# A Fourier transform fused with a soft mixture of experts: another order of the first phase's units

## The chip, the cores and the metric

The kernel runs on one core of a Trainium2 chip. The metric is the device time of one execution in microseconds (us); for a set of runs the median is given. The profiler records one further execution, and all views of the profile below come from that one.

## What is computed

The input `x` has the shape (8, 2496, 256). A two-dimensional discrete Fourier transform is taken over its last two axes and the real part kept; the 19968 rows of the result then go through a soft mixture of experts with 32 slots.

```python
X = np.fft.fft(np.fft.fft(x, axis=1), axis=2).real      # (8, 2496, 256)
x = X.reshape(19968, 256)
logits = x @ phi                                        # (19968, 32)
d = np.exp(logits - logits.max(0)); d /= d.sum(0) + 1e-9
slot_input = (d.T @ x).reshape(8, 4, 256)
for e in range(8):
    slot_out[e] = np.maximum(slot_input[e] @ w1[e], 0) @ w2[e]
c = np.exp(logits - logits.max(1)); c /= c.sum(1) + 1e-9
return c @ slot_out.reshape(32, 256)
```

The full transform is never formed. Only its product with `phi` is needed (2496 x 32 logits for each batch entry), and later the product of the softmax weights with it, so both transforms are applied to narrow matrices. 2496 is 64 x 39, and the transform along that axis is done in two steps, of length 64 and of length 39.

## The kernel before

The eight batch entries are worked on as four pairs, numbered 0 to 3. The work on a pair is cut into units, each a Python function with a letter; two digits behind the letter give the pair and the part. The list `ORDER` (line 34) names the units one after the other, and the loop at line 645 calls them in that order. The calls hand their instructions to a scheduling layer, which then puts the instructions of each engine in a queue; so `ORDER` sets the order of the queues broadly, and the layer may still move single instructions past each other. Every engine works through its queue strictly in order.

Two phases follow each other. The first phase, up to the unit `m00`, reads `x` and makes the logits and the slot inputs; its units are those that the change touches:

- `a` (`part_a`, line 209): one or two of the five loads `x` of a pair. VectorE (DVE) adds the halves of the load (lines 220 and 222) and forms its sum and difference into a tile `eo` (lines 224, 225). TensorE (PE) transposes `eo` in eight blocks into two banks `pt` (line 229), and ScalarE (ACT) copies each bank to a tile `et` (line 230). Unit parts 0 and 1 take two loads each, part 2 one.
- `z` (`part_z`, line 233): PE multiplies the `et` tiles of one `a` unit with `wphi` into a bank `z` (line 244), ACT copies it to `zs` (line 252).
- `t` (line 258): PE transposes the ten blocks of `zs` into `zt` (line 265), ACT copies.
- `b` (line 272): the transform of length 64, eleven products `a` of PE (line 279) and three copies of ACT into `o1` (line 286).
- `c` (line 288), in two halves: the transform of length 39, products `lp` and `lm` (lines 297, 298); ACT copies `lp` (line 299), DVE adds and subtracts `lm` to give the logits `lt` (lines 301, 302) and takes maxima (305). The maxima go through PE (`mt`, line 310), DVE (312, 314), PE again (`mt` out of `mex`, line 315) and DVE (317); then ACT takes the exponentials (320) and DVE forms `dpm` (322, 323).
- `e` (line 326) and `d` (line 346), in two halves each: the two transforms back, products at lines 335 and 353, copied by ACT (344, 359) and for one half of `d` by DVE (359).
- `u` (line 363): four products `tok` (line 366) and forty products with the `eo` tiles (line 376) into one bank `u`.
- `w` queues the loads of the experts' weights on SyncE (SP). They go into slots that `x` and `eo` tiles give up.

The second phase computes the experts (units `m`, `l`, `v`, `r`), the other softmax (`s`, `x`), and the output (`k`, `o`, `g`, `h`).

The products of PE are of different tile shapes, which matters below:

```python
pe.transpose(b[:, g * 128 : g * 128 + 128], e[:, g, k * 128 : k * 128 + 128], ident)   # 229 pt, whole array
z[32 * g : 32 * g + 32, o : o + n], ..., tile_position=(0, 32 * g),                    # 244 z, four strips of 32 columns
ps[64 * k : 64 * k + 64, 120 * i : 120 * i + 120], ..., tile_position=(0, 64 * k),     # 335 e, two halves of 64 columns
```

Using the whole array are `pt`, `zt`, `a`, `lp` and `lm`; four strips of 32 columns each take a part of `z`, `tok` and `u`; two halves of 64 columns take `e` and `d`; the transposes of the maxima `mt` (line 310) write 5 or 6 columns, and the transposes back (line 315) and the product `msel` (line 432) take 5 or 6 rows.

The buffers that bear on the order: `pt` and `z` share two PSUM banks (`P1 = 2`, tag `p1`); `zt`, `a`, `lp` and `lm` share two others (`P2 = 2`, tag `ps`); `mt`, `e`, `d` and `tok` share three (`P3 = 3`); `u` has one. There are three `et` tiles, six slots for `x` (`RING = 6`) and fifteen for `eo`.

Of the kernel before, what the change touches and what calls it, by code (L numbers as in the profile page):

```python
# [31 lines left out]
P1, P2, P3, PM = 2, 2, 3, 0  # L32
W2 = [1, 1, 1, 1, 1, 1, 1, 1, 1, 1, 1, 2, 2, 1]
ORDER = (
# [6 lines left out]
).split()  # L41


# [653 lines left out]
```

## Time and profile before

| | us |
|---|---|
| median of 3 runs | 194.75 |
| lowest and highest of them | 193.83, 195.87 |
| the profiled execution, its own time | 195.39 |
| the profiled execution, span from first to last instruction | 193.6 |
| mean granted clock of TensorE in it | 0.992 |

The time of an execution is a little longer than its span, here by 1.8 us. How much of the span each engine was busy, the span in 40 slices, and the waits are in the views that the prediction shows. To read them: PE is the matmuls of TensorE, PEld its weight loads, DVE VectorE, ACT ScalarE, POOL GpSimd, SP SyncE's queue. `pt<-cs,eo` is an instruction that writes `pt` and reads `cs` and `eo`. In the profile nearly every product of PE that is no transpose stands as two matmuls, so twelve products `z` are "x24", while four transposes `pt` are "x4". In the view of the chain each piece runs from the end of the piece before it to its own end.

### The profile page before, as it was taken

The page shows a single profiled execution, that of the slowest core. Times are in us where ns is not written, and L with a number is a line of the kernel's source. Part 1 is how long each engine was busy: PE and PEld are TensorE (multiplying, and loading weights), DVE is VectorE, ACT ScalarE, POOL GpSimd, SP SyncE. Part 2 cuts the span into 40 slices and gives each one's busy share as a digit, 9 for nine tenths or more (in the row PEclk, how much of TensorE's full clock was granted, in tenths as well). Part 3 has the DMA queues.
Part 4 walks back from the last instruction along what each step waited for, and adds up shares of the span by engine and source line. Part 5 has one row for each costly group of instructions (what it writes and reads, how often), then busy time and mean ns, then how long its engine had stood idle before and what let it go on. Part 6 is the DMA issues. An engine that isn't in the chain of part 4 may idle for free.

```text
span 193.6 us, 4203 instructions
## 1 busy us (share of the span) xinstructions
PE 170.0 (88%) x1682; PEld 108.1 (56%) x1682; DVE 125.3 (65%) x227; ACT 111.0 (57%) x244; POOL 20.9 (11%) x25
## 2 busy tenths in 40 slices
PE   0489899899999989999998999999998998988930
PEld 0376577578676876566873878256544443434410
DVE  0499877899995990742257653760489776985740
ACT  2132586586967485475762852521878595784630
POOL 0000000000000000000000000550054325522000
PEclk9999999999999999999999999999999999999996
DMA  5999999999980299700870698990199899999995
GB/s 179 401 428 411 419 416 422 423 414 413 352 325 7 59 413 416 300 3 3 260 278 8 192 346 273 400 406 20 70 405 368 327 406 413 354 422 397 417 427 229
DMA packets 10994, 59.16 MB, mean 306 GB/s; under 512 B 1376, under 2 KB 1760, under 8 KB 6240
## 3 DMA queue, kind: packets, MB, share of 16 engines
q1 hardware_dynamic: 10976, 58.91, 77.4%
q8 instruction: 13, 0.21, 0.5%
q14 instruction: 5, 0.04, 0.1%
HBM read 38.46 MB, written 20.45 MB: 304 GB/s over the span
## 4 chain that ended last, share of the span: by engine, by line
PE 78%; DVE 6%; ACT 5%; DMA 4%; issue 1%; SPq 1%; POOL 1%; ACTq 0%; DVEq 0%; POOLq 0%
PE po L610 18%; PE pt L229 9%; PE z L244 8%; PE e L335 7%; PE d L353 5%; PE a L279 5%; PE u L376 4%; PE h L477 4%; DMA phi<-phih 4%; PE so L497 4%; PE lT L591 3%; PE lp L297 2%; PE lm L298 2%; PE zt L265 2%; PE cT L530 2%; ACT et L230 2%
## 5 line engine op out<-in xcount | busy, mean ns | idle before, releaser
L610 PE MATMUL po<-rh,lTs 64*128 64x512 f32 x160 | 38.1, 607 | 2.2 <-ACT lTs L594 2.1
L618 DVE COPY o<-po 128x512 f32<-128x512 f32 (+1 forms) x40 | 26.8, 680 | 17.4 <-PE po L610 17.1
L229 PE MATMUL pt<-cs,eo 128*128 128x128 f32 x160 | 26.2, 301 | 7.8 <-DVE eo L224 7.6
L230 ACT COPY et<-pt 128x512 f32<-128x512 f32 x40 | 22.8, 587 | 15.4 <-PE pt L229 15.3
L618 ACT COPY o<-po 128x512 f32<-128x512 f32 x40 | 23.2, 585 | 12.1 <-PE po L610 12.1
L229 PEld LDWEIGHTS pt<-cs,eo 128*128 128x128 f32 x160 | 19.9, 153 | 14.2 <-DVE eo L224 7.6
L610 PEld LDWEIGHTS po<-rh,lTs 64*128 64x128 f32 x160 | 14.3, 186 | 17.0 <-issue 10.2
L222 DVE TENSOR_TENSOR x<-x 128x1024 f32<-128x1024 f32 x16 | 19.4, 1215 | 3.3 <-DMA x<-xh 3.3
L244 PE MATMUL z<-et,wphi 128*32 128x256 f32 (+1 forms) x288 | 16.8, 368 | 2.4 <-ACT et L230 2.4
L547 POOL TENSOR_TENSOR c<-c,cm 128x640 f32<-128x640 f32 x8 | 10.0, 1264 | 69.6 <-DVE cm L546 69.6
L320 ACT ACTIVATE d<-lt,nm 120x128 f32<-120x128 f32 x44 | 13.7, 391 | 3.6 <-DVE nm L317 3.6
L335 PE MATMUL e<-cs,dpm 120*64 120x120 f32 x176 | 13.9, 273 | 0.0
L224 DVE TENSOR_TENSOR eo<-x 128x512 f32<-128x512 f32 x20 | 13.6, 682 | 0.3
L225 DVE TENSOR_TENSOR eo<-x 128x512 f32<-128x512 f32 x20 | 13.6, 679 | 0.0
L244 PEld LDWEIGHTS z<-et,wphi 128*32 128x32 f32 x288 | 8.1, 114 | 9.3 <-ACT et L230 3.9
L335 PEld LDWEIGHTS e<-cs,dpm 120*64 120x64 f32 x176 | 11.4, 136 | 2.4 <-issue 1.8
L279 PE MATMUL a<-cs,zt 128*120 128x128 f32 x88 | 11.8, 279 | 1.0 <-DVE lt L302 0.9
L252 ACT COPY zs<-z 128x512 f32<-128x512 f32 (+1 forms) x12 | 6.2, 513 | 10.4 <-PE z L244 10.4
L376 PE MATMUL u<-eo,ds 128*32 128x129 f32 x320 | 11.5, 275 | 0.1
L557 POOL TENSOR_TENSOR c<-c,cm 128x640 f32<-128x640 f32 x8 | 10.1, 1264 | 13.7 <-DVE cm L556 9.5
L279 PEld LDWEIGHTS a<-cs,zt 128*120 128x120 f32 x88 | 10.4, 183 | 2.1 <-DVE lt L302 1.1
L353 PE MATMUL d<-e,cs 128*64 128x320 f32 x64 | 10.7, 443 | 0.5 <-ACT ds L359 0.5
(91 smaller groups left out, 218.5 us busy)
## 6 DMA issues: line engine op xcount, KB each, us to landing
x<-xh SPq DMA_DIRECT2D x16, 1024.0 KB, 12.3
out<-o SPq DMA_DIRECT2D x13, 1024.0 KB, 4.8
w<-w1h SPq DMA_DIRECT2D x6, 1024.0 KB, 8.2
w<-w2h SPq DMA_DIRECT2D x12, 512.0 KB, 6.5
x<-xh SPq DMA_DIRECT2D x4, 896.0 KB, 11.7
out<-o SPq DMA_DIRECT2D x4, 768.0 KB, 5.1
out<-o SPq DMA_DIRECT2D x5, 512.0 KB, 3.6
w<-w1h SPq DMA_DIRECT2D x4, 512.0 KB, 6.8
```

The costliest lines, as they stand in the source:

```text
L222: v.tensor_tensor(x[:, 0:4], x[:, 0:4], x[:, 4:8], op=ALU.add)
L224: v.tensor_tensor(e[:, :, 0:128], x[:, 0:4, 0:128], x[:, 0:4, 128:256], op=ALU.add)
L229: pe.transpose(b[:, g * 128 : g * 128 + 128], e[:, g, k * 128 : k * 128 + 128], ident)
L230: sc.copy(tr[k][:, :, :, qi, :], b.rearrange("p (g h a) -> p g h a", g=4, h=2))
L244: pe.matmul(z[32 * g : 32 * g + 32, o : o + n], wphi[:, w, :], tr[k][:, g].rearrange("p h q a -> p (h q a)"), start=w != 0, stop=w != 1, t ...
L279: pe.matmul(ps[:120, i * 128 : i * 128 + 128], zt[p][:, GS * g : GS * g + GS].rearrange("p s h c -> p (s h c)"), C("wa"), start=True, stop ...
L320: sc.activation(d[:, g], L[:, g], AF.Exp, bias=nm[:, g : g + 1], scale=1.0)
L335: pe.matmul(ps[64 * k : 64 * k + 64, 120 * i : 120 * i + 120], dpm[p, hf][:, k, 3 * j + i, :], C(name), start=True, stop=True, tile_positi ...
L353: pe.matmul(ps[64 * h : 64 * h + 64, :320], C("wb")[:, 64 * k : 64 * k + 64], esb[p].rearrange("p g (s h c) -> p (g s) h c", h=2, c=NKC)[: ...
L376: last = pe.matmul(ub[32 * g : 32 * g + 32, 0:129], dsb[p][:, k, c, :], e[:, 0:129] if k == 0 else e[:, 127:256], start=cc == 0, stop=cc == 9,
L610: ins = pe.matmul(po[h], lts[p, b, t][rows], rh[0][rows].rearrange("p k d -> p (k d)"), start=True, stop=True, tile_position=(64 * h, 0),)
L618: ins = ev(ot[:np_, 2 * i : 2 * i + 2, :].rearrange("p k d -> p (k d)"), po[h][:np_])
```

## The change

The list `ORDER` is written in another order up to the unit `u30`; what follows `m00` is the same, and so is every function. No unit is added or left out.

```diff
 ORDER = (
-    "a00 z00 a01 z01 a02 z02 t00 a10 z10 b00 a11 z11 c00 c01 e00 e01 d00 a12 z12 t10 a20 z20 a21 z21 "
-    "a22 z22 d01 b10 c10 e10 u00 a30 z30 d10 t20 c11 e11 b20 d11 c20 c21 a31 z31 "
...
+    "a00 z00 a01 a02 z01 z02 a10 t00 z10 b00 c00 c01 e00 d00 a11 a12 z11 z12 a20 e01 z20 d01 u00 t10 "
+    "b10 c10 a21 z21 c11 e10 d10 a22 z22 t20 a30 z30 b20 e11 c20 a31 d11 z31 c21 u10 a32 z32 t30 e20 "
...
 ).split()
```

In the pairs 0 and 1 the units `a` of parts 1 and 2 now stand together, and the units `z` of these parts behind them. Some units `c`, `e`, `d` and `u` of a pair move to other places between the units `a` and `z` of the next.

Three places show what this makes of the queues. In the names the digit straight behind the letters is the pair, the next one the load, half or part; the last number is a running number of the tile and can be passed over.

PE's queue in pair 0, between the loads 3 and 4 and the first transposes of pair 1, before:

```order
L229 MATMUL pt0_3_0_212<-cs0_70,eo0_3_143 128x128 x4
L229 MATMUL pt0_3_1_218<-cs0_70,eo0_3_143 128x128 x4
L244 MATMUL z0_1_224<-et0_1_1_193,wphi_100 32x256 x8
L244 MATMUL z0_1_224<-et0_1_0_192,wphi_100 32x256 x4
L229 MATMUL pt0_4_0_243<-cs0_70,eo0_4_144 128x128 x4
L229 MATMUL pt0_4_1_249<-cs0_70,eo0_4_144 128x128 x4
L265 MATMUL zt0_0_271<-cs0_70,zs0_177 128x128 x2
L265 MATMUL zt0_1_277<-cs0_70,zs0_177 128x128 x2
L244 MATMUL z0_2_255<-et0_2_1_239,wphi_100 32x128 x8
L244 MATMUL z0_2_255<-et0_2_0_238,wphi_100 32x128 x4
L229 MATMUL pt1_0_0_298<-cs0_70,eo1_0_288 128x128 x4
```

and in the changed kernel:

```order
L229 MATMUL pt0_3_0_212<-cs0_70,eo0_3_143 128x128 x4
L229 MATMUL pt0_3_1_218<-cs0_70,eo0_3_143 128x128 x4
L229 MATMUL pt0_4_0_229<-cs0_70,eo0_4_144 128x128 x4
L229 MATMUL pt0_4_1_235<-cs0_70,eo0_4_144 128x128 x4
L244 MATMUL z0_1_241<-et0_1_1_193,wphi_100 32x256 x8
L244 MATMUL z0_1_241<-et0_1_0_192,wphi_100 32x256 x4
L244 MATMUL z0_2_255<-et0_2_1_225,wphi_100 32x128 x8
L244 MATMUL z0_2_255<-et0_2_0_224,wphi_100 32x128 x4
L229 MATMUL pt1_0_0_279<-cs0_70,eo1_0_269 128x128 x4
```

The product `z` of part 1 has moved behind the transposes of load 4 and stands next to the `z` of part 2; two blocks `zt` that stood between them come later.

DVE's queue where the second half of pair 1's logits is formed, before:

```order
L224 TENSOR_TENSOR eo3_3_799<-x3_3_131 128x4x128
L225 TENSOR_TENSOR eo3_3_799<-x3_3_131 128x4x128
L317 COPY nm1_0_719<-mt1_0_713 120x6
L224 TENSOR_TENSOR eo3_4_800<-x3_4_133 128x4x128
L225 TENSOR_TENSOR eo3_4_800<-x3_4_133 128x4x128
L301 TENSOR_TENSOR lt1_703<-lt1_703,lm1_1_877 120x5x64
L302 TENSOR_TENSOR lt1_703<-lt1_703,lm1_1_877 120x5x64
```

and in the changed kernel:

```order
L302 TENSOR_TENSOR lt1_674<-lt1_674,lm1_0_676 120x6x64
L222 TENSOR_TENSOR x3_1_127<-x3_1_127 128x1024
L301 TENSOR_TENSOR lt1_674<-lt1_674,lm1_1_749 120x5x64
L322 TENSOR_TENSOR dpm0_1_409<-d0_1_403 120x320
L323 TENSOR_TENSOR dpm0_1_409<-d0_1_403 120x320
L305 TENSOR_REDUCE mx1_0_682<-lt1_674 120x6
L302 TENSOR_TENSOR lt1_674<-lt1_674,lm1_1_749 120x5x64
L359 COPY ds0_429<-d0_1_0_434 128x20x16
L222 TENSOR_TENSOR x3_2_129<-x3_2_129 128x1024
```

The two operations that empty the bank of `lm1_1` stood behind the whole preparation of pair 3; now they stand between pair 3's loads 1 and 2.

PE's queue at pair 3's transform of length 64 and of length 39, before:

```order
L279 MATMUL a3_1_1178<-cs2_72,zt3_1090 120x128 x4
L335 MATMUL e2_0_0_1043<-cs3_73,dpm2_0_967 64x120
L335 MATMUL e2_0_1_1051<-cs3_73,dpm2_0_967 64x120
L279 MATMUL a3_2_1184<-cs2_72,zt3_1090 120x128 x3
L335 MATMUL e2_0_0_1043<-cs3_73,dpm2_0_967 64x120 x5
L335 MATMUL e2_0_1_1051<-cs3_73,dpm2_0_967 64x120 x5
L297 MATMUL lp3_0_1199<-o13_1171,cs2_72 120x384
L298 MATMUL lm3_0_1200<-o13_1171,cs2_72 120x384
L335 MATMUL e2_1_0_1109<-cs3_73,dpm2_1_993 64x120
L335 MATMUL e2_1_1_1117<-cs3_73,dpm2_1_993 64x120
L335 MATMUL e2_1_0_1109<-cs3_73,dpm2_1_993 64x120 x5
L335 MATMUL e2_1_1_1117<-cs3_73,dpm2_1_993 64x120 x3
```

and in the changed kernel:

```order
L279 MATMUL a3_0_1158<-cs2_72,zt3_1121 120x128 x4
L279 MATMUL a3_1_1164<-cs2_72,zt3_1121 120x128 x4
L279 MATMUL a3_2_1170<-cs2_72,zt3_1121 120x128 x3
L297 MATMUL lp3_0_1240<-o13_1157,cs2_72 120x384
L298 MATMUL lm3_0_1241<-o13_1157,cs2_72 120x384
L297 MATMUL lp3_1_1284<-o13_1157,cs2_72 120x320
L298 MATMUL lm3_1_1285<-o13_1157,cs2_72 120x320
L310 MATMUL mt3_0_1249<-cs0_70,mx3_0_1247 6x120
L353 MATMUL d2_0_0_1268<-e2_1140,cs2_72 64x320 x2
L353 MATMUL d2_1_0_1272<-e2_1140,cs2_72 64x320 x2
```

The products `e` of pair 2, which stood between pair 3's products, have all moved ahead of them; pair 3's `a`, `lp` and `lm` follow each other without a break.

8 rows, old and new, of the table ORDER are left out of this document.

## The prediction

> **What bounds the kernel now.** I read the page first, for the engine that is busy throughout; then the busy times by stretch, for where it is; then the chain of waits in order of time, for what a change of tile shape costs; last the timeline of PE and the totals of the waits, for what PE waits for. The page:
>
> ```profile
> span 193.6 us, 4203 instructions
> ...
> PE 170.0 (88%) x1682; PEld 108.1 (56%) x1682; DVE 125.3 (65%) x227; ACT 111.0 (57%) x244; POOL 20.9 (11%) x25
> ...
> PE   0489899899999989999998999999998998988930
> ...
> DVE  0499877899995990742257653760489776985740
> ```
>
> PE is busy 88% of the span and in nearly every slice. DVE is as full only up to the fifteenth slice (72 us). The change ends at PE's first `cT` (117.6 us in the chain below); I split what lies ahead of that where the same PE work is done by both orders: behind pair 2's first `z` (49.2 us) and behind pair 3's first `z` (73.5 us). Columns: length, then busy time with the number of instructions for PE, PEld, DVE, ACT, POOL, then granted clock, DMA share, GB/s.
>
> ```profile
> 7.60:49.20 41.60, 38.69 (x353) 28.56 (x353) 36.36 (x55) 24.36 (x50) 0.26 (x2) 1.00 1.02 415
> 49.20:73.50 24.30, 23.44 (x297) 17.69 (x293) 21.32 (x36) 16.82 (x43) 0.13 (x1) 1.00 0.62 237
> 73.50:117.60 44.10, 43.00 (x591) 30.40 (x587) 19.98 (x54) 25.69 (x72) 0.00 (x0) 1.00 0.54 193
> 117.60:193.60 76.00, 64.91 (x452) 31.47 (x450) 45.94 (x81) 42.81 (x79) 20.09 (x16) 0.98 0.84 338
> ```
>
> In the first stage the loads run at 415 GB/s with the DMA engines full, and DVE, which must prepare each load, is busy 36.36 of 41.60 us: PE is fed. In the second, PE and DVE are both nearly full (23.44 and 21.32 of 24.30). In the third DVE has more than half its time free, and PE alone sets the pace (43.00 of 44.10). The fourth the change does not touch.
>
> PE's busy time hides a cost that the chain shows (start, length, what; each length is from end to end):
>
> ```profile
> 30.95 0.65 PE lp L297 x2
> ...
> 46.27 0.66 PE a L279 x6
> ...
> 51.58 0.44 PE pt L229 x4
> 52.02 0.55 PE e L335 x4
> 52.57 0.59 PE pt L229 x4
> 53.16 1.37 PE e L335 x20
> ...
> 92.08 1.02 PE u L376 x32
> ...
> 95.93 0.84 PE a L279 x6
> ...
> 98.15 0.83 PE lp L297 x2
> ...
> 101.75 0.54 PE lm L298 x2
> 102.29 1.23 PE d L353 x8
> 109.80 2.60 PE e L335 x42
> 112.40 2.27 PE d L353 x16
> 115.24 2.39 PE u L376 x76
> 117.63 0.56 PE cT L530 x4
> ```
>
> The same four transposes take 0.44 us behind other whole-array work and 0.59 behind an `e`: a change of shape costs 0.15. Likewise `a`: 0.84 - 0.66 = 0.18; `lp`: 0.83 - 0.65 = 0.18. For the others I compare a short group with a long one. `e`: 22 matmuls more cost 2.60 - 1.37 = 1.23, or 56 ns each; so 20 would take 1.12, and entering costs 0.25; for the group of four 0.55 - 0.22 = 0.33. `d`: eight more cost 1.04, so entering costs 1.23 - 1.04 = 0.19. `u`: 44 more cost 1.37, 31 ns each, so 32 take 1.00 and entering seems free by this; since that division has a rounding of its own, I bound it by 0 and by the 0.19 of `d`, and take the middle, 0.10, for all strips.
>
> The Trainium skill, "TensorEngine Tiling (Array Packing)", section "Key Properties", says that changing the tiling mode, not just the tile, drains the TensorE. This trace agrees in direction (0.59 against 0.44 us). The page gives no price; "TensorE: Matmul & The Clock Gate", section "Step-by-step: what each phase is for", puts the drain at about 128 cycles, 53 ns at 2.4 GHz, so an estimate from that page for 14 changes would be -0.7 us. The rows above measure more.
>
> What PE waits for, in the timeline (the last bracket is the idle time before, and who ended it), and the waits in total:
>
> ```profile
> 21.73 1.50 PE L244 MATMUL z<-et,wphi 128*32 128x256 f32 x24 [0.73 <-ACT et L230]
> 25.32 0.86 PE L244 MATMUL z<-et,wphi 128*32 128x128 f32 x24 [0.29 <-ACT et L230]
> 37.33 1.50 PE L244 MATMUL z<-et,wphi 128*32 128x256 f32 x24 [0.68 <-ACT et L230]
> 71.26 0.92 PE L279 MATMUL a<-cs,zt 128*120 128x128 f32 x6 [0.86 <-DVE lt L302]
> 82.13 0.22 PE L315 MATMUL mt<-cs,mex 5*120 5x5 f32 x1 [0.17 <-DVE mex L314]
> 82.62 0.41 PE L265 MATMUL zt<-cs,zs 128*128 128x128 f32 x2 [0.27 <-DVE nm L317]
> 101.59 0.70 PE L298 MATMUL lm<-o,cs 120*120 120x320 f32 x2
> 104.93 0.76 PE L353 MATMUL d<-e,cs 128*64 128x320 f32 x4 [0.52 <-ACT ds L359]
> ...
> 20.60 1.07 ACT L230 COPY et<-pt 128x512 f32<-128x512 f32 x2 [0.61 <-PE pt L229]
> 34.84 0.43 ACT L299 COPY lt<-lp 120x320 f32<-120x320 f32 x1 [0.60 <-PE lp L297]
> ...
> DVE lt L301 <- PE lm L298: 8.9, 5, 5.0
> ...
> PEld h L477 <- DMA w<-w2h: 0.9, 3, 0.3
> ```
>
> **The change, part by part.** It adds and removes no instruction. I went down PE's queue and counted the rows whose kind of tile differs from the row before (whole array; strips; halves; `mt`; transposes back and `msel`), as far as the first `cT`: 85 changes before, 71 now. By stage 21 and 17, 18 and 20, 46 and 34.
>
> *First stage.* Four changes less: at `pt` three, at `z`, `zt` and `lp` one each, against two more at `a`; 3 x 0.15 + 0.10 + 0.15 + 0.18 - 2 x 0.18 = 0.52 us of PE's work. The waits of `z` for ACT's copies in pairs 0 and 1 (0.73 and 0.68) go too, since the transposes of load 4 now stand between. But those transposes now follow load 3's straight on. They share two banks, ACT needs 1.07 / 2 = 0.54 us to empty one and PE 0.44 to fill one, so PE waits there some 0.1 each time; and the second `z` straight behind the first must wait for an `et` tile, of which there are three: the copy into it (0.54) starts only when the first `z` has read the old content, so some 0.5 where 0.29 was. The `zt` blocks and pair 1's next transposes stand behind these copies and come late by 0.3 to 0.4 each. More important, the loads and DVE give the pace of this stage, and neither starts sooner: an `x` slot is freed by DVE alone, and DVE's queue over pairs 0 and 1 starts the same. I take this stage at 0, with bounds -0.5 and +0.5.
>
> *Second and third stage.* Ten changes less (64 to 54): at `a` two less, `lm` two, `e` two, and at the strips six (`z` one, `u` two, `tok` three); one more at `pt` and at `d`. That is 0.36 + 0.36 + 2 x 0.29 (middle of 0.25 and 0.33) + 6 x 0.10 - 0.15 - 0.19 = 1.56 us off PE's work. If entering the strips is free it is 0.96; at 0.19 it is 2.10.
>
> Waits that go: the 0.86 us at 71.26, because DVE now empties pair 1's last `lm` bank before it prepares the end of pair 3 and not after; 0.17 + 0.27 at 82, because pair 1's maxima are done earlier; and 0.52 at 104.93, where `d` waited for ACT's copy of the bank before, and now a transpose and `msel` stand between. Sum 1.82.
>
> Waits that come: pair 3's `a`, `lp` and `lm` now follow each other without the `e` that stood between. They have two banks, so a product waits for the copy of the one before the last. The second `lm` waits for the second `lp` to end (0.70, taken from the `lm` of the same size at 101.59) and for ACT's copy of it (0.43), less the 0.54 in which PE is done with it in the chain (row 101.75): 0.6. The same reckoning at the first `lp` and the second `lp`, where more stands between, gives 0.1 to 0.2 each; and `mt` behind them waits for DVE's chain on that `lm`, some 0.4. Sum 1.3. All of it is on the path, as PE alone sets the pace there. What hid it before, twelve products `e`, is used up earlier.
>
> Sum: 0 - 1.56 - 1.82 + 1.3 = -2.1 us. The last stage moves up with it: its weight loads are issued when `u` gives up its `eo` tiles, and the `u` units move up as well, so I cost the SP queue at nothing; the weights' cover would be gone if the last loads arrived later than their products, and now the longest wait for them is 0.3 us (last row above). The sum stands against the profiled execution's own 195.39 us (span 193.6), which is 0.6 above the median: 193.3 there, and 194.75 - 2.1 = 192.6 on the median.
>
> **The rivals.** *The new waits eat most of it.* In the first stage and at pair 3, units that share two banks now follow each other. If at pair 3 each of the three waits for a copy finds ACT just taken by another of 0.43, that is 1.3 more: -0.8, 193.9. For it speaks that ACT's copy (0.54) is longer than PE's group (0.44); against it that ACT is busy only 25.69 of 44.10 us in the third stage. The Trainium skill, "Perfetto Trace Analysis", section "Matmuls", bears on it: independent matmul groups should rotate through different banks so that the emptying of one overlaps the next group. With two banks that is just met, and no run here shows yet what a third would give.
>
> *The gain is larger.* If the first stage does keep its 0.52 and the waits of `z` (1.41), because DVE has 5.2 us free in it, then -2.1 - 1.9 = -4.0: 190.7. For it: PE's busy share there is 93%. Against it: a DMA share of 1.02.
>
> *Slower.* DVE's additions for pair 1's logits now stand ahead of pair 3's additions in its queue, so if PE brings `lm` late, DVE stands still with pair 3's loads behind it. DVE's waits for `lm` were 8.9 us in five, the longest 5.0. DVE has 24.30 - 21.32 = 3.0 us free in the second stage; from a wait of 3.0 on, the rest is on the path. With one of 5.0 that is +2.0, and the 1.82 of waits come back: -2.1 + 3.8 = +1.7, 196.5. Against it: pair 1's second `lm` now stands well ahead in PE's queue, before that pair's `mt`.
>
> That the change doesn't do what it says is excluded: the queues show 14 changes of shape less, and the chain that a change has a price.
>
> **How the numbers follow.** The forecast has 0.60, the first rival 0.22, the larger gain 0.12, the slower case 0.06. What a measurement of this kernel can tell from no change is about 1%, 1.9 us: under 192.8 is faster, over 196.7 slower. The forecast's own range is 191.4 to 193.9 (strips free or at 0.19; first stage at -0.5 or +0.5), and somewhat more than half of it lies under 192.8: 0.34. With the larger gain and a little of the first rival that is 0.48 faster; slower is the upper half of the slow case, 0.04; the same 0.48. To leave two in ten out, the range takes in the first rival and part of the larger gain: 191.2 to 194.5.
>
> **What would show it.** In the profile after: the transposes of load 4 in pairs 0 and 1 without a `z` ahead of them, and those `z` without idle time before them; the second `z` of pair 0 with about 0.5 us idle; no wait of `a` for `lt`; at pair 3 the second `lm` with about 0.6 us idle. The stretch from pair 2's first `z` to the first `cT`, 68.4 us now, should be 66.3. If instead the stretch up to pair 2's first `z`, 41.6 us, is shorter by more than 1 us, the first stage was not set by loads and DVE; if idle time at pair 3 exceeds 2 us, the first rival holds; if DVE shows a wait for `lm` over 3 us between pairs 1 and 3, the slow one.

## The result, and the profile after

The changed kernel takes 192.24 us (median of 4 runs, 191.79 to 192.42), the kernel before 195.08 (4 runs, 193.83 to 195.87): ratio 0.985, 95% interval 0.981 to 0.989. Each median here and below is over all executions of a kernel, while the ratios leave out those more than 1.5% above its fastest (one of 4 of `u_whole`, three of 12 of `h4_start_alone`, and five of 12 of `b1_third_bank`, whose profile is of one of the five). The profiled execution of the changed kernel took 191.79 us with a span of 190.0. Its page:

```profile
span 190.0 us, 4194 instructions
...
PE 166.9 (88%) x1682; PEld 104.8 (55%) x1682; DVE 125.9 (66%) x227; ACT 110.8 (58%) x244; POOL 20.9 (11%) x25
```

PE does the same 1682 instructions in 3.1 us less busy time (it was 170.0). Where, the busy times of the changed kernel by stretch show (columns as in the prediction; cut behind pair 2's first `z`, behind pair 3's first `z`, and at the first `cT`):

```profile
7.70:48.50 40.80, 37.90 (x353) 27.54 (x353) 36.38 (x55) 24.43 (x51) 0.27 (x2) 1.00 1.02 418
48.50:72.20 23.70, 23.57 (x310) 17.20 (x306) 20.85 (x38) 16.75 (x45) 0.13 (x1) 1.00 0.62 222
72.20:114.00 41.80, 40.46 (x578) 28.61 (x574) 20.00 (x53) 25.50 (x72) 0.00 (x0) 1.00 0.59 218
114.00:190.00 76.00, 64.98 (x453) 31.50 (x450) 46.95 (x81) 42.87 (x79) 20.12 (x16) 0.98 0.84 338
```

The first stage is 0.8 us shorter than before, the second 0.6, the third 2.3, the last the same. The second cut is not at the same work: in the changed kernel twelve products (eight `tok`, two `lp`, two `mt`) have moved from the third stage into the second, so these two can only be read together, and the same holds for what the prediction and some expectations say of them singly. In the second and third together PE is busy 64.03 us where it was 66.44, that is 2.41 less, and idle 1.47 where it was 1.96, that is 0.49 less. Most of the gain is thus in PE's own rows, not in its waits. By line, the groups of PE in these two stages, first before and then after (busy us, mean ns of one, idle time ahead):

```profile
L335 PE MATMUL e<-cs,dpm 120*64 120x120 f32 x176 | 13.9, 273 | 0.0
L376 PE MATMUL u<-eo,ds 128*32 128x129 f32 x320 | 11.5, 275 | 0.1
...
L279 PE MATMUL a<-cs,zt 128*120 128x128 f32 x44 | 6.2, 283 | 0.9 <-DVE lt L302 0.9
```

```profile
L335 PE MATMUL e<-cs,dpm 120*64 120x120 f32 x176 | 12.3, 272 | 0.1
L376 PE MATMUL u<-eo,ds 128*32 128x129 f32 x320 | 11.2, 275 | 0.1
...
L279 PE MATMUL a<-cs,zt 128*120 128x128 f32 x44 | 5.5, 276 | 0.0
```

The products themselves are no faster (273 and 272 ns); `e` alone lies in fewer pieces and takes 1.6 us less, `a` 0.7, `u` 0.3.

The waits of PE in the changed kernel's timeline:

```profile
21.22 1.50 PE L244 MATMUL z<-et,wphi 128*32 128x256 f32 x24 [0.15 <-ACT et L230]
23.05 0.86 PE L244 MATMUL z<-et,wphi 128*32 128x128 f32 x24 [0.33 <-ACT et L230]
25.67 0.44 PE L265 MATMUL zt<-cs,zs 128*128 128x128 f32 x2 [0.29 <-ACT zt L267]
42.66 0.48 PE L279 MATMUL a<-cs,zt 128*120 128x128 f32 x2 [0.74 <-ACT zt L270]
...
90.96 0.44 PE L265 MATMUL zt<-cs,zs 128*128 128x128 f32 x2 [0.38 <-ACT zs L252]
98.11 0.80 PE L298 MATMUL lm<-o,cs 120*120 120x320 f32 x2 [0.52 <-ACT lt L299]
99.17 0.27 PE L310 MATMUL mt<-cs,mx 120*6 120x120 f32 x1 [0.26 <-DVE mx L305]
```

The wait of `a` for `lt` (0.86), those at 82 us and that of `d` (0.52) are gone. New in the third stage are a wait of `zt` for ACT's copy to `zs` (0.38) and, at pair 3, those of the second `lm` and the `mt` behind it, 0.52 and 0.26.

### The profile page after: what moved, and what is told of

Read it like the earlier page. It is cut to its first block, busy times and chain, and to the rows that moved or that the text cites. A ratio compares the mean times of both kernels' runs of the same rounds, so it can differ in the third digit from the quotient of the medians.

```text
span 190.0 us, 4194 instructions
## 1 busy us (share of the span) xinstructions
PE 166.9 (88%) x1682; PEld 104.8 (55%) x1682; DVE 125.9 (66%) x227; ACT 110.8 (58%) x244; POOL 20.9 (11%) x25
## 4 chain that ended last, share of the span: by engine, by line
PE 73%; ACT 12%; DVE 5%; DMA 3%; issue 2%; POOL 1%; SPq 0%; ACTq 0%; DVEq 0%; POOLq 0%
PE po L610 18%; PE pt L229 9%; PE z L244 8%; PE a L279 6%; PE d L353 5%; ACT d L320 4%; PE h L477 4%; PE e L335 4%; PE so L497 4%; ACT et L230 3%; PE u L376 3%; PE lT L591 3%; DMA x<-xh 3%; PE lp L297 2%; PE lm L298 2%; PE cT L530 2%
## 5 line engine op out<-in xcount | busy, mean ns | idle before, releaser
L229 PE MATMUL pt<-cs,eo 128*128 128x128 f32 x160 | 25.7, 293 | 8.1 <-DVE eo L224 7.7
L229 PEld LDWEIGHTS pt<-cs,eo 128*128 128x128 f32 x160 | 19.3, 149 | 13.9 <-DVE eo L224 7.7
L335 PE MATMUL e<-cs,dpm 120*64 120x120 f32 x176 | 12.3, 272 | 0.1
L335 PEld LDWEIGHTS e<-cs,dpm 120*64 120x64 f32 x176 | 10.1, 136 | 2.5 <-issue 0.8
```

Source lines behind the costliest of these rows:

```text
L335: pe.matmul(ps[64 * k : 64 * k + 64, 120 * i : 120 * i + 120], dpm[p, hf][:, k, 3 * j + i, :], C(name), start=True, stop=True, tile_positi ...
```

## The experiments

For the kernels that move units alone, the table shows changes of shape up to the first `cT`, the stretch from pair 2's first `z` to the first `cT` in the profiled execution, and a split of it: I took the usual time from the start of one product to the start of the next, which makes 53.26 us in every kernel; what the first and last products at a change of shape take beyond that is "changes", all else "waits". The split is my reckoning from the start times in the traces.

| kernel | changes of shape | stretch, us | of it changes, waits | ratio to before (95% interval) |
|---|---|---|---|---|
| before | 85 | 68.29 | 12.07, 2.96 | |
| the changed kernel | 71 | 65.49 | 9.80, 2.43 | 0.985 (0.981 to 0.989) |
| h1_group_alone | 85 | 68.92 | 11.90, 3.76 | 1.006 (1.004 to 1.008) |
| h2_no_group | 76 | 65.92 | 10.50, 2.16 | 0.987 (0.985 to 0.989) |
| h3_rest_alone | 77 | 67.87 | 10.65, 3.96 | 1.003 (0.999 to 1.006) |
| h4_start_alone | 81 | 68.04 | 11.09, 3.69 | 1.005 (1.001 to 1.009) |
| h6_e_back | 67 | 66.17 | 8.92, 3.99 | 0.994 (0.991 to 0.997) |
| s1_other_order | 72 | 64.55 | 9.05, 2.24 | 0.990 (0.985 to 0.994) |

**The price of a change, by itself.** Nine products of one column in the shape of the whole array were put into pair 3's `u`, between its ten groups of four products; they write a column that nobody reads, and the copy of `tok` moves behind them. The control has the same nine in the shape of `u`.

```diff
             for cc in range(10):
+                if cc and p == NPAIR - 1:
+                    with tc.issue_after(last.ins):
+                        last = pe.matmul(ps[:, 8:9], ident, C("onehot"), start=True, stop=True)
```

> The changed kernel with nine added small products (one column each) in pair 3's u, one ahead of each group of four u products but the first, in whole-array shape; they write an unused column. Nothing else stands in PE's queue there. Theory 'price of a change of shape': each of them brings two changes, 18 in all, at 0.10 to 0.19 us each, so pair 3's u takes 1.8 to 3.4 us longer than with the same nine products in strip shape. Rival 'shape is free, only waits count': no more than 0.3 us longer than with strips.

> The control: the changed kernel with the same nine added small products at the same places of pair 3's u, but in the shape of one strip, as u itself has. Both theories: only their own issue, some 0.05 us each, 0.3 to 0.9 us in all above the changed kernel.

> As u_whole, but three of the one-column products in the shape of the whole array inside pair 3's u, not nine: 6 changes of shape more where u_whole had 18. u_whole lengthened pair 3's u by 4.3 us against its control, or 0.24 us for a change with its share of the product, and ran slower for some 12 us behind it at a granted clock of 0.58. Theory 'price': pair 3's u is 1.2 to 1.5 us longer than the changed kernel's, and the clock behind it stays at 1.00: ratio 0.990 to 0.995. Rival 'the clock falls after any such product': the stretch behind is longer too, by 2 us or more: ratio 1.003 to 1.015. Rival 'changes inside the strips are nearly free and u_whole's length was the lower clock already': +0.3 us, ratio 0.986 to 0.988.

The control took 193.21 us (ratio 0.989, 0.986 to 0.991), `u_whole` 201.54 (1.031, 1.028 to 1.034), and `u3_whole_sparse`, with three such products (at `cc` 2, 5 and 8), 194.46 (0.996, 0.993 to 0.998). From `tok` to the first `cT` the changed kernel takes 2.93 us, the control 3.29. The timelines of `u3_whole_sparse` and of `u_whole` there:

```profile
111.33 0.24 PE L366 MATMUL tok<-cs,ds 128*32 128x1 f32 x8
...
112.50 0.38 PE L374 MATMUL tok<-cs,cs 128*128 128x1 f32 x2
...
115.61 0.63 PE L534 MATMUL cT<-cs,lt 120*128 120x120 f32 x4
```

```profile
111.98 0.24 PE L366 MATMUL tok<-cs,ds 128*32 128x1 f32 x8
...
117.62 0.38 PE L374 MATMUL tok<-cs,cs 128*128 128x1 f32 x2
...
118.44 0.59 PE L374 MATMUL tok<-cs,cs 128*128 128x1 f32 x2
...
119.55 1.06 PE L534 MATMUL cT<-cs,lt 120*128 120x120 f32 x4
```

Three products lengthen it to 4.28 us, nine to 7.57. Without the 0.36 / 9 = 0.04 us that each takes in the control, that is (1.35 - 0.12) / 6 = 0.20 us a change with six changes, and (7.57 - 3.29) / 18 = 0.24 with eighteen, whose 4.28 us are above the 1.8 to 3.4 expected. The 0.24 holds a lower clock: the last of the nine takes 0.59 us where the one before it takes 0.38, and the granted clock is 0.76 on the mean of 116 to 120 us (last section). The 0.20 is an upper bound, since a product may take longer by itself in the shape of the whole array than in that of one strip, where the control has it. In the lines of `u3_whole_sparse`,

```profile
L374 PE MATMUL tok<-cs,cs 128*128 128x1 f32 x6 | 1.1, 260 | 0.0
```

its two matmuls take 0.26 us each and 0.38 together, so the second starts some 0.12 behind the first, with no change of shape between. With 0.12 for each of the two, (0.45 - 0.24) / 2, about 0.1, is left for a change. Between 0.1 and 0.2 the price stays open; that only waits count (at most 0.3 us for eighteen) falls either way. The other half of the 8.3 us between `u_whole` and its control lies behind this stretch (last section).

**Which part of the order gains.** In `h1_group_alone` the kernel before has only the units `a` of parts 1 and 2 of pairs 0 and 1 together, and their `z` behind them; `h2_no_group` is the changed kernel without that. `h3_rest_alone` has before's order of the units up to the first `u` and the new order of the rest, `h4_start_alone` the reverse.

```diff
-h1: a00 z00 a01 z01 a02 z02 t00 a10 z10 b00 a11 z11 c00 c01 e00 e01 d00 a12 z12 t10
+h1: a00 z00 a01 a02 z01 z02 t00 a10 z10 b00 a11 a12 z11 z12 c00 c01 e00 e01 d00 t10
-h2: a00 z00 a01 a02 z01 z02 a10 t00 z10 b00 c00 c01 e00 d00 a11 a12 z11 z12 a20 e01
+h2: a00 z00 a01 z01 a02 z02 a10 t00 z10 b00 c00 c01 e00 d00 a11 z11 a12 z12 a20 e01
```

> The kernel before with only the grouping put in: in pairs 0 and 1 the units a of parts 1 and 2 stand together and their z behind them; c, e, d and u stay where they were. PE's queue then has 85 changes of shape, as before. Theory 'the grouping of a and z is what gains': 1 us or more below before, under 194. Theory 'the number of changes of shape and the waits of the whole queue count': no gain, 194.5 to 197, as other units fall between others.

> The changed kernel without the grouping: a01 z01 a02 z02 and a11 z11 a12 z12 again, the rest of the new order kept. 76 changes of shape against 71. Theory 'the grouping of a and z is what gains': back to about before, 194.5 to 195.5. Theory 'changes of shape and waits of the whole queue': most of the gain stays, 192.5 to 193.3 (five changes at 0.10 to 0.19, 0.5 to 0.9 us above the changed kernel).

> The kernel before, with the order of its units up to the first u kept, and only the rest (from pair 1's t on) in the new order: 77 changes of shape up to the first cT where the kernel before has 85 and the changed one 71. Theory 'price': 8 changes at about 0.16 us are -1.3 us against the kernel before, about 193.7, ratio 0.993. Rival 'the rest is where the gain is made' (the changed kernel's third stage is 2.2 us shorter than before): about -2.2, 192.9, ratio 0.989. Rival 'the order fits only as a whole' (each half leaves PE waiting for copies and loads that the other half would have brought earlier): within 0.5 us of the kernel before, ratio 0.998 to 1.003.

> The counterpart: the new order up to the first u, and the old order of what is left: 81 changes of shape. Theory 'price': -0.6 us against the kernel before, ratio 0.997. Rival 'the stages add up' (the first two stages of the changed kernel are 0.80 and 0.64 us shorter than before): -0.8 to -1.4, ratio 0.993 to 0.996. Rival 'the order fits only as a whole': -0.2 to +0.6, ratio 0.999 to 1.003.

By the whole time neither the grouping nor either half of the order gains anything by itself: 196.36, 195.82 and 196.84 us. Without the grouping the changed kernel keeps nearly all of its gain (192.66). In the stretch the grouping loses 0.63 us, and the halves keep 0.42 and 0.25 of the 2.80 that the whole order gains. The table says why: each does take something off the changes of shape (0.2, 1.4 and 1.0 us), and each brings waits (0.8, 1.0 and 0.7). The stretch doesn't explain why the whole times of the halves lie above that of the kernel before. For `h3_rest_alone` a lower clock in the last stage bears on it (last section); of `h4_start_alone`, the profiled execution took 194.39 us, like two more of its twelve, and the other nine took 196.3 to 197.3 us, which stays open. The timelines of `h1_group_alone`, of `h3_rest_alone` and of `h4_start_alone` name the waits:

```profile
52.07 1.14 PE L229 MATMUL pt<-cs,eo 128*128 128x128 f32 x8 [0.75 <-ACT et L230]
53.69 0.44 PE L265 MATMUL zt<-cs,zs 128*128 128x128 f32 x2 [0.48 <-DVE lt L302]
70.72 1.14 PE L229 MATMUL pt<-cs,eo 128*128 128x128 f32 x8 [0.56 <-ACT et L230]
```

```profile
55.83 1.50 PE L244 MATMUL z<-et,wphi 128*32 128x256 f32 x24 [0.46 <-ACT et L230]
73.35 1.50 PE L244 MATMUL z<-et,wphi 128*32 128x256 f32 x24 [1.06 <-ACT et L230]
```

```profile
85.32 0.86 PE L244 MATMUL z<-et,wphi 128*32 128x128 f32 x24 [1.08 <-ACT et L230]
...
103.98 0.76 PE L353 MATMUL d<-e,cs 128*64 128x320 f32 x4 [0.53 <-ACT ds L359]
```

Most are waits of `pt` and `z` for ACT's copies to `et`. That the transposes of a load and the `z` on it come too close where old order meets new is how I read these rows; it was not tried by itself. The rival that the order fits only as a whole comes nearest in both halves, and the price alone (-1.3 and -0.6 us) fails as a forecast of the time.

**Fewer changes at the price of waits.** `h6_e_back` puts pair 2's `e` back between pair 3's `b` and `c`, which makes four changes of shape fewer than in the changed kernel.

```diff
-a32 z32 t30 e20 b30 e21 w00 c30 d20 d21 c31 u20
+a32 z32 t30 b30 e20 c30 w00 e21 c31 d20 d21 u20
```

> The changed kernel with the e of pair 2 put back behind pair 3's b and between its two c, and d of pair 2 behind them: only 67 changes of shape where the changed kernel has 71. It keeps PE supplied with other work where the changed kernel waits for the copies of lp (about 1.4 us of waits that came), but zt, a and the first c of pair 3 now follow each other straight on. Theory 'price': 4 changes fewer at about 0.2 us are -0.8 us against the changed kernel, and part of the waits that came goes too, so ratio to the kernel before 0.976 to 0.981. Rival 'waits decide': the a of pair 3 then wait about 1 us for the copies of zt and the first products tok about 1 us for the copies of d, so +1.2 us against the changed kernel, ratio 0.990 to 0.993.

193.75 us, ratio 0.994: slower than the changed kernel, as the rival said, though in the stretch by 0.68 us where it had 1.2. By the table the changes cost 0.88 us less and the waits 1.56 more. In its timeline the wait of `lm` that the `e` was to hide is still there, and two new ones stand beside it:

```profile
92.09 2.72 PE L279 MATMUL a<-cs,zt 128*120 128x128 f32 x22 [0.62 <-ACT zt L270]
97.56 0.80 PE L298 MATMUL lm<-o,cs 120*120 120x320 f32 x2 [0.52 <-ACT lt L299]
...
104.86 0.24 PE L366 MATMUL tok<-cs,ds 128*32 128x1 f32 x8 [0.83 <-ACT ds L359]
```

**The same queue with twelve changes fewer.** In `w1_wide_mt` the transposes `mt` and back are 72 wide, over padding of zeros, and so no longer fit into half of the 128 columns.

```diff
-            pe.transpose(ps[:n, :120], mx, ident[:120, :120])
+            pe.transpose(ps[:WD, :120], mxw, ident[:120, :120])
...
-            pe.transpose(ps[:120, 128 : 128 + n], mex.rearrange("p s k -> p (s k)"), ident[:n, :n])
+            pe.transpose(ps[:120, 128 : 128 + WD], mexw.rearrange("p s k -> p (s k)"), ident[:WD, :WD])
```

> The changed kernel with the same queue of PE, but the twelve transposes of the maxima and back (mt) that write 5 or 6 columns or read 5 or 6 rows made 72 wide by padding the tiles with zeros, which are set once on GpSimd: these products then have the shape of the whole array like the products around most of them, and 12 of the 71 changes of shape go without anything being moved. Theory 'price' at 0.16 us each: -1.9 us against the changed kernel, ratio to the kernel before about 0.975. Rival 'an mt is paid for by a wait anyway' (most mt are waited for: the maxima of VectorE end after PE has come to them, and the wider product takes longer): within 0.4 us of the changed kernel, ratio 0.983 to 0.987.

191.55 us (191.43 to 193.89), ratio 0.986 (0.981 to 0.991); the stretch is 65.15 us, 0.34 less than the changed kernel's for twelve changes. The theory of a price of 0.16 for each change falls here; the rival's size holds. Whether the wider product's own time takes the gain, or a wait that stands there anyway, or whether a narrow `mt` costs no change of shape to begin with, these runs don't part. The counts of changes in the table hold such `mt`, so they are not a measure of time by themselves.

**A better order, and a third bank.** `s1_other_order` moves four units of the changed kernel once more, mainly pair 2's first `d` ahead of pair 3's first `c`; `s2_other_order_wide` adds the wide `mt`. `b1_third_bank` gives the changed kernel a third bank for `zt`, `a`, `lp` and `lm`, out of the three of `mt`, `e`, `d` and `tok`.

```diff
-s1: ... a11 a12 z11 z12 a20 e01 z20 ... t20 a30 z30 b20 e11 c20 a31 ... w00 c30 d20 d21 c31
+s1: ... a11 e01 a12 z11 z12 a20 z20 ... t20 b20 a30 z30 c20 a31 e11 ... w00 d20 c30 d21 c31
-b1: P1, P2, P3, PM = 2, 2, 3, 0
+b1: P1, P2, P3, PM = 2, 3, 2, 0
```

> The changed kernel with four units moved once more: pair 2's b ahead of pair 3's first a, pair 2's first d ahead of pair 3's first c (so that the copies at pair 3 have other work beside them), pair 0's second e and pair 1's second e a place earlier or later. 72 changes of shape, one more than the changed kernel. Theory 'price': +0.2 us against the changed kernel, ratio to the kernel before 0.986. Theory 'waits of the whole queue', worked out with the pitches and copy times of the traces: the waits of pair 3's first lp and first lm go, about -0.9 us against the changed kernel, ratio 0.980 to 0.982.

> The order of s1_other_order with the maxima's transposes 72 wide as in w1_wide_mt: 60 changes of shape. Theory 'price': -1.8 us against s1_other_order. Theory 'an mt is paid for by a wait': within 0.4 us of s1_other_order, as w1_wide_mt was within 0.7 us of the changed kernel; ratio to the kernel before 0.978 to 0.982.

> The changed kernel with one PSUM bank given from the three of mt, e, d and tok to the two of zt, a, lp and lm. The scheduling layer follows the pools, so the queue of PE changes with it: 77 changes of shape. Theory 'the waits that came are the two banks' (first rival's ground): the waits of lp and lm at pair 3, about 1.0 us, go and little comes: -1 us against the changed kernel, ratio to the kernel before 0.980. Rival 'the banks are all in use': e, d and tok wait for their copies in the place of lp and lm, most at pair 1's e behind pair 3's transposes, and the gain of the change is given back: ratio 0.998 to 1.012.

`s1_other_order` shortens the stretch by 0.94 us against the changed kernel, the size that its theory of the waits had. Its ground was another: the table puts 0.75 of it to the changes (9.05 against 9.80), with one change more by count, and 0.19 to the waits. Its time, 193.14 us, doesn't show it, since the granted clock fell in its tail (last section). `s2_other_order_wide` has the same stretch, 64.55, and the best time of all: 190.77 us (189.80 to 192.56), ratio 0.979 (0.973 to 0.984). It beats the kernel before; against the changed kernel the intervals overlap. With the third bank the gain of the change is gone: 196.75 us, ratio 1.006 (1.002 to 1.009). The timeline, of an execution of 200.36 us whose granted clock was 0.89 between 70 and 85 us, has no wait of `lp` or `lm`, and in their place

```profile
81.37 1.06 PE L335 MATMUL e<-cs,dpm 120*64 120x120 f32 x4 [2.10 <-DVE dpm L322]
...
109.66 0.24 PE L366 MATMUL tok<-cs,ds 128*32 128x1 f32 x8 [0.54 <-DVE ds L359]
```

The longer one is a wait of `e` for its input `dpm` from DVE, and not for a bank, as the expectation had it; the queue of PE is another one too (77 changes). So the run shows that this split of the banks, with the queue that comes with it, gives the gain away, and it doesn't show what a third bank would do to the same queue. The page that the first rival drew on (the Trainium skill, "Perfetto Trace Analysis", section "Matmuls") asks that independent matmul groups rotate through different banks, so that the emptying of one overlaps the next group. Two banks do that here, with 0.52 us of idle time left at pair 3's second `lm` in the changed kernel.

## Why the prediction was right, and where it was off

*The sum.* Forecast 192.6 us, 191.2 to 194.5; measured 192.24. In the stretch that it named, 68.4 us became 65.5 where it said 66.3.

*The waits* were sized rightly in their sum: -1.82 + 1.3 = -0.5 forecast, -0.49 by the idle time of PE, -0.53 by the split. The second `lm` of pair 3 idles 0.52 where 0.6 was said, the `mt` behind it 0.26 where 0.4 was said, the second `z` of pair 0 0.33 where 0.5 was said, and no `a` waits for `lt`. That the sum comes so close is in part luck: the 0.1 to 0.2 at each `lp` of pair 3 don't show as idle time, and the 0.38 of `zt` at 90.96 was not foreseen. In the first stage the `z` of pair 0's part 1 keeps 0.15 us, which was to be nothing. Not foreseen there were the 0.74 us of `a` at 42.66 and the 0.29 of `zt`, both behind copies of ACT.

*The price of the changes* is the term that was mis-sized: -1.56 forecast, -2.41 by PE's busy time, -2.27 by the split. The step that failed is the division of a long group less a short one, which gave 56 ns for a matmul of `e` and 31 for one of `u`. Groups that nothing cuts have shorter steps in the changed kernel's timeline:

```profile
57.80 1.30 PE L335 MATMUL e<-cs,dpm 120*64 120x120 f32 x20
86.08 1.30 PE L376 MATMUL u<-eo,ds 128*32 128x129 f32 x40
87.46 1.09 PE L376 MATMUL u<-eo,ds 128*32 128x129 f32 x32
105.47 1.50 PE L335 MATMUL e<-cs,dpm 120*64 120x120 f32 x24
```

Four more matmuls of `e` take 0.20 us and eight more of `u` 0.21, or 50 and 26 ns each. With these the rows of the prediction give 0.35 to 0.37 us for entering a piece of `e`, where 0.25 to 0.33 was taken, and 0.19 for `u`, where the strips got 0.10, the middle between nothing and 0.19. And an `e` that other work cuts in two costs more than its second entry. The chain of the changed kernel has, without and with a cut ahead of the twenty,

```profile
57.87 1.23 PE e L335 x20
...
73.47 0.56 PE e L335 x4
...
74.76 1.37 PE e L335 x20
```

so the cut `e` takes 0.56 + 1.37 = 1.93 us, and an uncut one of 24 some 1.23 + 4 x 0.050 = 1.43: 0.50 for a cut, where 0.29 was taken. Before, four halves of `e` were cut, now two. I also reckoned by kind, from end to end as in the chain, without the idle time and with each matmul at its usual step in the traces (51 ns for `e`, 27.5 for `u`): the halves of 64 columns (`e` and `d`) take 1.35 us less than before, the strips 0.94 less, and the groups of the whole array the same. The prediction had 0.39, 0.60 and 0.57 less. So most of what it missed lies at `e`. The 0.57 did not come because at pair 3 `a`, `lp` and `lm` together take 0.7 us more than their steps and one entry, time that the view counts as busy; that these are short waits for the two banks is not shown.

*The first stage* was taken at 0 and came out 0.8 us shorter in the profiled execution. That is less than the 1 us that would have spoken against it, and no gain can be read from it: six kernels with the new order up to pair 2's first `z` take 40.72, 40.83, 40.85, 41.04, 41.53 and 42.15 us there, the kernel before 41.63, and `h3_rest_alone`, which differs from it only in its last rows there, 41.10. The scatter has a cause that differs from one execution to the next (last section). Where PE came to its full pace latest, in `u_strip` with the new order and in the kernel before, the stage takes 42.15 and 41.63 us, so there the new order is not the shorter one.

*The rivals.* That new waits eat the gain did not happen here (1.34 us idle in the third stage, below the 2 us named), but in the stretch it is what happened to `h1_group_alone`, `h3_rest_alone` and `h4_start_alone`. There it was the copies to `et` more than the two banks at pair 3 that the rival named. The larger gain, by the first stage, isn't shown. The slow case is out: DVE's rows in the changed kernel's timeline,

```profile
77.37 0.49 DVE L301 TENSOR_TENSOR lt<-lt,lm 120x320 f32<-120x320 f32 x1 [0.97 <-PE lm L298]
96.98 0.56 DVE L301 TENSOR_TENSOR lt<-lt,lm 120x384 f32<-120x384 f32 x1 [5.57 <-PE lm L298]
```

have at most 0.97 us of waiting for `lm` ahead of pair 3; the 5.57 stands at pair 3 itself, with no load left to prepare behind it.

## What to carry to other kernels

By the chains, entering another tile shape on TensorE costs about 0.15 to 0.37 us here, and cutting a group in two 0.5, so units of one shape belong together, but only where the copies between them keep their distance: reckon the changes and the waits, and judge an order as a whole. Half of a good order kept 0.25 and 0.42 of its 2.80 us. Equal counts of changes don't mean equal time: twelve narrow ones were worth 0.34 us together. When an engine is the bound, read the gain in its busy time as well as in its idle time, since a change of shape stands in the profile as busy.

## What was not expected of the hardware

**PE reaches its full pace at another time in each execution.** The timelines of before, of the changed kernel and of `u_strip`, at the same transposes of pair 0:

```profile
17.34 1.97 PE L229 MATMUL pt<-cs,eo 128*128 128x128 f32 x8
19.10 1.03 PE L265 MATMUL zt<-cs,zs 128*128 128x128 f32 x4
```

```profile
16.90 1.44 PE L229 MATMUL pt<-cs,eo 128*128 128x128 f32 x8
18.18 0.60 PE L265 MATMUL zt<-cs,zs 128*128 128x128 f32 x4
```

```profile
17.29 1.97 PE L229 MATMUL pt<-cs,eo 128*128 128x128 f32 x8
19.05 1.06 PE L265 MATMUL zt<-cs,zs 128*128 128x128 f32 x4
```

`u_strip` has the same queue as the changed kernel here and yet the slow transposes of before; its first stage is 42.15 us. The Trainium skill, "TensorE: Matmul & The Clock Gate", section "What's actually happening", says that the array runs at half rate until about 3.4 us of sustained work, in a window that doesn't start with the kernel, so that the point varies. The variation agrees, and so does the factor, roughly (1.03 and 0.60). The 3.4 us don't: PE's first transposes start at 7.65 to 7.77 us in these three, so the full pace comes 9 to 12 us later, with PE busy 8.43 us of the 10 between 7 and 17 us in the kernel before. The granted clock of the profile stands at 1.00 over all of it and doesn't show it.

**The granted clock falls while PE is busy.** From the end of the eighteen added changes on, `u_whole` has in its windows (the last three columns are clock, DMA share, GB/s)

```profile
116.00:120.00 4.00, 4.00 (x50) 2.60 (x51) 0.48 (x3) 0.16 (x1) 0.00 (x0) 0.76 0.92 300
120.00:130.00 10.00, 10.00 (x59) 5.32 (x61) 3.70 (x13) 3.19 (x6) 2.48 (x2) 0.58 0.60 218
```

with PE busy throughout, and its tail, from the first `cT` to the end, is 79.75 us against the control's 76.02. All four of its executions have a mean granted clock of 0.946 to 0.968, the control's 0.988 to 0.995. With six changes, in `u3_whole_sparse`, the clock stays at 1.00 there. What sets it off isn't settled. A shorter fall, in the last stage, comes in some executions of several kernels; the windows of `s1_other_order` and of the changed kernel:

```profile
170.00:175.00 5.00, 3.56 (x12) 1.45 (x12) 2.69 (x5) 1.17 (x2) 1.92 (x2) 0.73 0.98 401
```

```profile
170.00:175.00 5.00, 3.21 (x18) 1.58 (x18) 3.50 (x7) 2.02 (x4) 2.27 (x2) 1.00 1.00 413
```

The tail of `s1_other_order` is 77.61 us against 75.95. Of the other profiled executions, those of `h3_rest_alone`, `h6_e_back`, `s2_other_order_wide` and `u3_whole_sparse` have 77.55 to 77.60 us at a mean granted clock of 0.977 to 0.979, and six more 75.94 to 76.05 at 0.986 to 0.992, which is why the stretch ahead of it tells the orders apart better than the whole time does.
